# A transformer block, forward and backward: output accumulators without a memset, and a rearranged stage between the forward and the backward attention

## Chip, cores, metric

The kernel runs on one core of one Trainium2 chip. The metric is the time of one execution in device microseconds (us); lower is better. A kernel of 3.0 ms is built from about 72,000 instructions on five engines: TensorE (PE in the profile; its weight loads are PEld), VectorE (DVE), ScalarE (ACT), GpSimd (POOL) and SyncE (SP, which issues transfers).

## The reference

One block of a transformer with adaptive layer norm, for 2048 positions, width 512, 32 heads of 16 and a hidden width of 1792, in bf16. The kernel computes the output and the gradients of nine inputs.

```python
def _A_ref(x, wqkv, wo):                       # attention
    q, k, v = ...                              # (x @ wqkv), 32 heads of 16
    p = _softmax(jnp.einsum('bhqd,bhkd->bhqk', q, k) * 16 ** -0.5)
    return merge_heads(jnp.einsum('bhqk,bhkd->bhqd', p, v)) @ wo

def _B_ref(x, w1, b1, w2, b2):                 # MLP with a squared relu
    r = jnp.maximum(x @ w1 + b1, 0)
    return (r * r) @ w2 + b2

sa, ca, ga, sb, cb, gb = split(_silu(c) @ w_mod, 6)
h = _layernorm(x) * (1 + ca) + sa
x = x + ga * _A_ref(h, A_wqkv, A_wo)
h = _layernorm(x) * (1 + cb) + sb
x = x + gb * _B_ref(h, B_w1, B_b1, B_w2, B_b2)
# returned: x, and the vjp of all this with grad_out
```

The gradients that the change touches are those of w1 and w2 (dW1 and dW2), of b1 (db1: 1792 numbers) and of the modulation vectors sb and cb, which are sums over dW1's blocks.

## The kernel before

It works in three parts. A forward attention, with the MLP of earlier chunks of 512 positions worked in between its units; a middle, in which the last chunk's MLP is done forward and backward and then dW1 and dW2 are formed; and the backward of the attention.

In the forward, a unit is 16 blocks of keys for 512 queries and two heads. Its products are summed in PSUM, the memory that TensorE's matmuls write, in one of two accumulators, which take turns. Both are halves of one tile, `accbank`.

```python
        accbank = accp.tile([P, 2, 2, 4, DH + 1], F32, name="accbank")
        # ...
        def pv(u):
            (qc, g, jp, kb, acc, pu) = u          # acc = accbank[:, n % 2]
            if kb == 0:
                nc.vector.memset(acc, 0.0)                                            # L324
            for a in range(2):
                h = 4 * g + 2 * jp + a
                for sub in range(4):
                    nc.tensor.matmul(acc[:, a, sub, :], lhsT=pu[:, a, sub * P:(sub + 1) * P],
                                     rhs=Vaug[:, kb, h, :], start=False, stop=False,
                                     skip_group_check=True)                           # L328
            if kb < ST - 1:
                return
            for a in range(2):                    # evacuation, after the last block of keys
                nc.vector.reciprocal(self.rl[...], acc[:, a, :, DH])                  # L335
                nc.vector.tensor_tensor(O32[...], acc[:, a, :, 0:DH], ..., ALU.mult)  # L336
```

In the middle, four slices of 128 positions go through `dx` (the gradient in front of the MLP), `fc2` (the MLP's output) and `do` (the gradient in front of the attention's last product). `do` loads a slice of the attention's output, `o32`, through GpSimd's queue and multiplies with it on VectorE.

```python
        def dx(k):
            # ... 14 matmuls
            dx1 = mk.tile([P, D], F32, name="dx1")              # one buffer
            self.ln_bwd_tile(mk, pt[:], xh[:, k, :], gt4[:, k, :], rstd[:, k:k + 1], dx1[:])
            nc.sync.dma_start(tm_v(self.dx1_d)[:, k, :], dx1[:])
            # ... a bf16 copy dxb, stored too; turn_dx(k) transposes it on TensorE
        for k in range(4):
            dx(k)
            if k: turn_dx(k - 1)
            if k > 1: turn_do(k - 2)
            fc2(k)
            if k: do(k - 1)
        # ... dW1 (14 blocks) and dW2 (14 blocks) are worked in between and drained
        self.open_bwd()                     # memsets of 8 masked tiles, first loads of the backward
        fill.drain()
        db1_b = w1p.tile([P, FT], BF16, name="db1_b", bufs=1)
        nc.vector.tensor_copy(db1_b[:], self.db1[:])
        with nc.allow_non_contiguous_dma(reason="column-layout store"):
            nc.gpsimd.dma_start(io["out_5"].rearrange("(t p) -> p t", p=P), db1_b[:])
```

The last line is the store of db1. Its tile has position p on partition p and 14 numbers in a row, and in memory neighbours of such a row are 128 numbers apart: every piece of the transfer is a single number of 2 bytes. It stands at the end of the program text, but it needs only `db1`, and it is issued early, at 1220.7 us (dW2 starts at 1338.0).

A block of dW1, with the sums for the modulation vectors:

```python
            # 64 matmuls into g4 (128 x 512), then the column sums csb of du (one more matmul)
            nc.scalar.copy(csb, csb_ps[:, :P])
            nc.gpsimd.tensor_tensor(t1[:], csb.unsqueeze(1).to_broadcast([P, DT, P]), sbT_b, ALU.mult)
            nc.vector.tensor_tensor(t2[:], g4[:], opcb_b, ALU.mult)
            nc.vector.tensor_tensor(t3[:], g4[:], w1_blk[:], ALU.mult)
            nc.vector.tensor_tensor(dw1[:], t2[:], t1[:], ALU.add)
            nc.gpsimd.dma_start(dw1_v[:, :, ft * P:(ft + 1) * P], dw1[:])
            nc.gpsimd.tensor_tensor(acc_cb[:], acc_cb[:], t3[:], ALU.add)
        # after the 14 blocks: w1 is loaded once more (w1k) for 16 products with csb
```

The softmax here doesn't subtract the row's maximum and nothing guards it: scores larger than these inputs give would overflow.

## Time and profile before

| | us |
|---|---|
| time, median of the runs beside the changed kernel | 3084.86 |
| span of the profiled execution | 3069.6 |
| last exponential of the forward starts | 1148.6 |
| dx stage starts (end of the last product before it) | 1195.0 |
| dW2 starts | 1338.0 |
| backward's first VectorE product starts | 1401.4 |

The last four rows are places in the timeline. Two lines of the page's part on the costliest groups carry the forward. Columns: line, engine, operation, out and in, shapes and count; then busy us and ns of one; then the idle time in front of it and what ended most of that.

```profile
L361 ACT ACTIVATE pu<-st 128x1024 bf16<-128x1024 f32 x1024 | 956.8, 1047 | 84.4 <-PE st L358 80.4
...
L328 PE MATMUL accbank<-Vaug,pu 128*128 128x17 bf16 x8192 | 359.3, 171 | 70.0 <-DVE accbank L324 64.1
```

ScalarE, which sets the pace (between 450 and 750 us it works 285 of 300 us, TensorE 275), stands idle 84.4 us in front of its exponentials, nearly all of it for scores from TensorE. TensorE waits 70.0 us in front of the products into the accumulator, 64.1 of them for the memset.

In the middle, the transfers of the dx stage (view of the transfers, 1195 to 1260 us; columns: what, queue, count, size of one, median us from issue to landing):

```profile
dx_d<-dx SPq DMA_DIRECT2D x4, 256.0 KB, 2.5
...
o<-O_d POOLq DMA_DIRECT2D x3, 256.0 KB, 4.9
...
out_dram<-db_b POOLq DMA_DIRECT2D x1, 3.5 KB, 20.7
```

### The profile page before, as it was taken

What the parts mean: (1) busy time and instruction counts of PE and PEld (TensorE: products, weight loads), DVE (VectorE), ACT (ScalarE), POOL (GpSimd) and SP (SyncE); (2) the same over time, 40 slices, a digit from 0 to 9 for tenths busy, and PEclk for the clock granted to TensorE, in tenths of its full rate; (3) what the DMA queues carried; (4) which work ended last, traced back from release to release, by engine and by line L of the source; (5) the groups of instructions that cost most, each with busy time, mean ns of one, the idle gap of its engine ahead of it and who ended that gap; (6) DMA issues with size and microseconds to landing.
All of it is one profiled execution on the core that took longest, in us unless ns stands there. A gap on an engine that the chain in (4) does not pass through costs nothing. (4 is left out here: it accounts for less than half of the span.)

```text
span 3069.6 us, 72394 instructions
## 1 busy us (share of the span) xinstructions
PE 2731.8 (89%) x29893; PEld 1417.4 (46%) x30394; DVE 1822.7 (59%) x2661; ACT 2240.1 (73%) x3322; POOL 396.6 (13%) x646
## 2 busy tenths in 40 slices
PE   3689889989998988589999999999999999999796
PEld 1345445544444543454444444444444444444343
DVE  5322123322322334367888888888888888888575
ACT  3489999999999984106777777777777777777443
POOL 2343111320221122571000000000000000000000
PEclk7899999999999999799999999999999999999898
DMA  3974230531351136888999999999999999999942
GB/s 128 212 166 121 65 88 25 141 80 37 93 114 48 54 99 183 177 195 164 188 205 200 188 204 189 201 194 192 205 191 206 195 194 206 188 188 180 235 128 72
DMA packets 1306719, 471.12 MB, mean 153 GB/s; under 512 B 1237074, under 2 KB 1269844, under 8 KB 1306388
## 3 DMA queue, kind: packets, MB, share of 16 engines
q1 hardware_dynamic: 1277476, 378.87, 65.7%
q0 software_dynamic: 28384, 86.01, 9.1%
q8 instruction: 238, 3.90, 0.5%
q10 hardware_dynamic: 528, 1.57, 0.1%
q14 instruction: 93, 0.76, 0.1%
HBM read 88.87 MB, written 67.64 MB: 51 GB/s over the span
## 5 line engine op out<-in xcount | busy, mean ns | idle before, releaser
L1185 ACT ACTIVATE pu<-st 128x512 bf16<-128x512 f32 x2048 | 1132.7, 597 | 361.0 <-PE st L1183 297.4
L1190 DVE TENSOR_TENSOR ds<-dp,pu 128x1024 bf16<-128x1024 f32 x1024 | 1208.1, 1219 | 232.9 <-ACT pu L1185 225.0
L361 ACT ACTIVATE pu<-st 128x1024 bf16<-128x1024 f32 x1024 | 956.8, 1047 | 84.4 <-PE st L358 80.4
L1183 PE MATMUL st<-KTm,QTq 128*128 128x512 bf16 x2048 | 778.3, 380 | 13.3 <-ACT pu L1185 11.5
L1133 PEld LDWEIGHTS <-dsT 128*128 128x128 bf16 x8192 | 486.7, 96 | 489.6 <-DMA dsT<-ds 20.2
L1186 PE MATMUL dp<-VTm,dOTq 128*128 128x512 bf16 x1779 | 672.6, 378 | 7.4 <-DVE ds L1190 6.0
L358 PE MATMUL st<-QTm,KTq 128*128 128x512 bf16 x1937 | 596.0, 384 | 57.9 <-issue 17.4
L1133 PE MATMUL accq<-Kg,dsT 128*128 128x16 bf16 x8192 | 493.2, 170 | 27.8 <-DMA dsT<-ds 13.5
L328 PEld LDWEIGHTS <-pu 128*128 128x128 bf16 x8192 | 355.7, 96 | 326.1 <-issue 95.9
L328 PE MATMUL accbank<-Vaug,pu 128*128 128x17 bf16 x8192 | 359.3, 171 | 70.0 <-DVE accbank L324 64.1
L1113 PE MATMUL acckv<-ds,Qg 128*16 128x512 bf16 x2048 | 308.3, 381 | 0.9 <-DVE ds L1190 0.7
L1113 PE MATMUL acckv<-pu,dOg 128*16 128x512 bf16 x2048 | 308.3, 381 | 0.0
L1183 PEld LDWEIGHTS <-QTq 128*128 128x128 bf16 x2048 | 195.9, 96 | 220.8 <-issue 215.8
L358 PEld LDWEIGHTS <-KTq 128*128 128x128 bf16 x2048 | 194.7, 97 | 214.7 <-issue 165.4
L1186 PEld LDWEIGHTS <-dOTq 128*128 128x128 bf16 x2048 | 197.3, 96 | 38.0 <-DVE ds L1190 16.2
L1044 POOL DMA_DIRECT2D wqkv<-in_A_wqkv_dram x1 | 0.8, 788 | 1493.1 <-DMA dsT<-ds 1493.1
L464 DVE TENSOR_SCALAR ev_fm<-pps,bcol 128x512 bf16<-128x512 f32 x60 | 45.0, 750 | 156.7 <-PE pps L456 88.7
L335 DVE RECIPROCAL rl<-accbank 128x4 f32<-128x4 f32 x128 | 23.0, 179 | 175.3 <-PE accbank L328 175.3
L309 POOL DMA_DIRECT2D QTm<-QTq_d x128 | 64.9, 510 | 450.0 <-PE st L358 406.4
L914 DVE TENSOR_SCALAR rT<-pps,bias 128x512 bf16<-128x512 f32 x42 | 31.5, 750 | 116.9 <-PE pps L911 116.7
L922 DVE SCALAR_TENSOR_TENSOR auT<-pps,rT 128x512 bf16<-128x512 f32 x42 | 29.0, 691 | 86.1 <-PE pps L920 71.0
L456 PE MATMUL pps<-xhat1T,wpad 128*128 128x512 bf16 x223 | 78.8, 393 | 0.3 <-issue 0.2
(313 smaller groups left out, 2125.1 us busy)
## 6 DMA issues: line engine op xcount, KB each, us to landing
KTq<-KTq_d POOLq DMA_DIRECT2D x32, 512.0 KB, 3.6
duT_d<-auT POOLq DMA_DIRECT2D x4, 1792.0 KB, 8.2
aT_d<-rT POOLq DMA_DIRECT2D x4, 1792.0 KB, 12.7
QTq_d<-ev_fm SPq DMA_DIRECT2D x32, 128.0 KB, 2.1
QTm<-QTq_d POOLq DMA_DIRECT2D x128, 32.0 KB, 2.0
KTq_d<-ev_fm SPq DMA_DIRECT2D x32, 128.0 KB, 2.0
VTq_d<-vT POOLq DMA_DIRECT2D x4, 1024.0 KB, 6.3
O_d<-O POOLq DMA_DIRECT2D x4, 1024.0 KB, 7.1
```

What stands on the lines that cost most here:

```text
L309: nc.gpsimd.dma_start(QTm[j][32 * j:32 * j + 32, :], self.QTq_d[g, 32 * j:32 * j + 32, 512 * qc:512 * (qc + 1)])
L328: nc.tensor.matmul(acc[:, a, sub, :], lhsT=pu[:, a, sub * P:(sub + 1) * P], rhs=Vaug[:, kb, h, :], start=False, stop=False, skip_group_che ...
L358: nc.tensor.matmul(stt[:, a, :], lhsT=KT[:, kb * P:(kb + 1) * P], rhs=QTm[2 * jp + a][:], start=True, stop=True)
L361: nc.scalar.activation(pu[:], stt[:], ACT.Exp, scale=self.scale)
L456: nc.tensor.matmul(pt[:], lhsT=self.wpads[t][:, kt, g, :], rhs=self.xhat1T[:, kt, s0:s0 + 512], start=(kt == 0), stop=(kt == DT - 1))
L464: nc.vector.tensor_scalar(ev[:], pt[:], bc, None, ALU.add)
L1113: nc.tensor.matmul(acckv[r:r + DH, :], lhsT=T[n][:, ib, col:col + DH], rhs=src[:, a, :], start=(ib == 0), stop=(ib == ST - 1))
L1133: nc.tensor.matmul(accq[:, ib, a, :], lhsT=dsT[:, (i * 2 + a) * 4 + sub, :], rhs=T["K"][:, 4 * c + sub, col:col + DH], start=(c == 0 and i ...
L1183: nc.tensor.matmul(stt[:], lhsT=T["QT"][:, q], rhs=masked["KT"][2 * jp + a][:, c0:c0 + 512], start=True, stop=True)
L1185: nc.scalar.activation(pu[:, a, :], stt[:], ACT.Exp, scale=self.scale)
L1186: nc.tensor.matmul(dp[:, a, :], lhsT=T["dOT"][:, q], rhs=masked["VT"][2 * jp + a][:, c0:c0 + 512], start=True, stop=True)
L1190: nc.vector.tensor_tensor(dsg[:, i], dp[:], pu[:], ALU.mult)
```

## The change

Its intent: take the memset out of the way of the forward's products; keep the operands of dW1 and dW2 resident from the last chunk's MLP on, instead of loading them again; give the dx stage four slices of dx1 and a looser order; do the dW1 epilogue (the work on a block after its matmuls) with per-partition scalars on VectorE and ScalarE, without GpSimd and without the second load of w1; load dW1's blocks three ahead instead of two; and issue the backward's first loads later. The stores of dx1 also move from SyncE's queue to GpSimd's.

```diff
-            if kb == 0:
-                nc.vector.memset(acc, 0.0)
...
-                                     start=False, stop=False, skip_group_check=True)
+                                     start=(kb == 0 and a == 0 and sub == 0), stop=False, skip_group_check=True)
... (loads: resident g_tm and xh2 for dW2 and dW1)
+        nc.sync.dma_start(xh2[:, :st0, :], self.xhat2_d.rearrange("(st p) d -> p st d", p=P)[:, :st0, :])
+        nc.sync.dma_start(g_tm[:, :st0, :], io["grad_out"][0].rearrange("(st p) d -> p st d", p=P)[:, :st0, :])
... (dx stage)
-            dx1 = mk.tile([P, D], F32, name="dx1")
-            self.ln_bwd_tile(mk, pt[:], xh[:, k, :], gt4[:, k, :], rstd[:, k:k + 1], dx1[:])
-            nc.sync.dma_start(tm_v(self.dx1_d)[:, k, :], dx1[:])
+            dx1 = dx1s[:, k, :]
+            self.ln_bwd_tile(mk, pt[:], xh[:, k, :], gt4[:, k, :], rstd[:, k:k + 1], dx1)
+            nc.gpsimd.dma_start(tm_v(self.dx1_d)[:, k, :], dx1)
... (order: dx0 dx1 fc2_0 turn dx2 do0 fc2_1 turn dx3 turn do1 fc2_2 ... in place of the loop; then)
         self.open_bwd()
+        while fill.mark != "half":     # half of dW2
+            fill.next()
+        self.load_bwd()                # the backward's first loads
         fill.drain()
... (dW1: three blocks loaded ahead instead of two; epilogue)
-            nc.gpsimd.tensor_tensor(t1[:], csb.unsqueeze(1).to_broadcast([P, DT, P]), sbT_b, ALU.mult)
-            nc.vector.tensor_tensor(t2[:], g4[:], opcb_b, ALU.mult)
-            nc.vector.tensor_tensor(t3[:], g4[:], w1_blk[:], ALU.mult)
-            nc.vector.tensor_tensor(dw1[:], t2[:], t1[:], ALU.add)
+            for kt in range(DT):
+                nc.scalar.activation(t1[:, kt, :], csb[:], ACT.Copy, scale=self.mod_col(3)[:, kt:kt + 1])
+                nc.vector.scalar_tensor_tensor(dw1[:, kt, :], g4[:, kt, :], self.opcbT[:, kt:kt + 1], t1[:, kt, :], ALU.mult, ALU.add)
+                nc.vector.scalar_tensor_tensor(junk[:], g4[:, kt, :], 1.0, w1_blk[:, kt, :], ALU.mult, ALU.mult,
+                                               accum_out=dcb_part[:, kt, ft:ft + 1])
+                nc.vector.scalar_tensor_tensor(junk2[:], csb[:], 1.0, w1_blk[:, kt, :], ALU.mult, ALU.mult,
+                                               accum_out=dsb_part[:, kt, ft:ft + 1])
... (the w1k loads with their 16 products are gone; in dW2)
-            tmp = sb.tile([P, D], F32, name="g2w2", bufs=1)
+            tmp = sb.tile([P, D], F32, name="g2w2")          # two buffers
```

More of the change, by code (lines that the diff above doesn't have):

```diff
@@ L582, in last_chunk @@
             x0s.append(t)
-        gt4 = e0.tile([P, 4, D], BF16, name="gt4")
-        nc.sync.dma_start(gt4[:], tm_v(io["grad_out"][0]))
         x1 = e0.tile([P, 4, D], F32, name="x1_l")
+        g_tm = e0.tile([P, ST, D], BF16, name="g_tm")
+        xh2 = e0.tile([P, ST, D], BF16, name="xh2")
+        gt4, xh = g_tm[:, st0:, :], xh2[:, st0:, :]
         OT = mk.tile([P, 4, DT, P], BF16, name="fT", bufs=2)
@@ L588, in last_chunk @@
         nc.sync.dma_start_transpose(gT[:], io["grad_out"][0, s0:s0 + 512, :])
+        nc.sync.dma_start(gt4, tm_v(io["grad_out"][0]))
+        nc.sync.dma_start(xh2[:, :st0, :], self.xhat2_d.rearrange("(st p) d -> p st d", p=P)[:, :st0, :])
+        nc.sync.dma_start(g_tm[:, :st0, :], io["grad_out"][0].rearrange("(st p) d -> p st d", p=P)[:, :st0, :])
         bg.take(15)
@@ L597, in last_chunk @@
         nmr = mk.tile([P, 4], F32, name="nmr")
-        xh = mk.tile([P, 4, D], BF16, name="xh2")
         for k in range(4):
@@ L611, in last_chunk @@
         bg.drain()
-        nc.gpsimd.dma_start(tm_v(self.xhat2_d), xh[:])
         xhT = mk.tile([P, 4, DT, P], BF16, name="fT", bufs=2)
@@ L636, in last_chunk @@
         w1p = self.open_pool("dw1", bufs=2)
-        xh2 = w1p.tile([P, ST, D], BF16, name="xh2", bufs=1)
-        nc.sync.dma_start(xh2[:], self.xhat2_d.rearrange("(st p) d -> p st d", p=P))
         fill = Background()
@@ L641, in last_chunk @@
         dxTs, dOpads = {}, {}
+        dx1s = mk.tile([P, 4, D], F32, name="x1")
         def dx(k):
@@ L647, in dx @@
                                  start=(ft == 0), stop=(ft == FT - 1))
-            dx1 = mk.tile([P, D], F32, name="dx1")
-            self.ln_bwd_tile(mk, pt[:], xh[:, k, :], gt4[:, k, :], rstd[:, k:k + 1], dx1[:])
-            nc.sync.dma_start(tm_v(self.dx1_d)[:, k, :], dx1[:])
+            dx1 = dx1s[:, k, :]
+            self.ln_bwd_tile(mk, pt[:], xh[:, k, :], gt4[:, k, :], rstd[:, k:k + 1], dx1)
+            nc.gpsimd.dma_start(tm_v(self.dx1_d)[:, k, :], dx1)
             dxb = mk.tile([P, D], BF16, name="dxb", bufs=2)
-            nc.scalar.copy(dxb[:], dx1[:])
+            nc.scalar.copy(dxb[:], dx1)
             nc.gpsimd.dma_start(tm_v(self.dx1b_d)[:, k, :], dxb[:])
@@ L681, in fc2 @@
             nc.gpsimd.dma_start(tm_v(io["out_0"][0])[:, k, :], o[:])
-        for k in range(4):
-            dx(k)
-            if k:
-                turn_dx(k - 1)
-            if k > 1:
-                turn_do(k - 2)
-            fc2(k)
-            if k:
-                do(k - 1)
+        dx(0)
+        dx(1)
+        fc2(0)
+        turn_dx(0)
+        dx(2)
+        do(0)
+        fc2(1)
+        turn_dx(1)
+        dx(3)
+        turn_do(0)
+        do(1)
+        fc2(2)
+        turn_dx(2)
+        turn_do(1)
+        fc2(3)
+        do(2)
         self.close_pool("mlp_f")
-        g_tm = self.open_pool("dw2", bufs=2)
-        fill.add(self.gen_dw2(g_tm))
-        fill.take(16)
+        w2p = self.open_pool("dw2", bufs=2)
+        fill.add(self.gen_dw2(w2p, g_tm))
+        fill.take(4)
         turn_dx(3)
+        fill.take(4)
         turn_do(2)
-        fill.take(4)
         do(3)
-        fill.take(24)
+        fill.take(32)
         turn_do(3)
@@ L718, in gen_dw1 @@
         dw1_v = io["out_4"].rearrange("(kt p) f -> p kt f", p=P)
-        db1_bc = sb.tile([P, F], F32, name="db1_bc", bufs=1)
-        acc_cb = sb.tile([P, DT, P], F32, name="acc_cb", bufs=1)
-        nc.gpsimd.memset(acc_cb[:], 0.0)
-        opcb_b = self.opcbT[:].unsqueeze(2).to_broadcast([P, DT, P])
-        sbT_b = self.mod_col(3).unsqueeze(2).to_broadcast([P, DT, P])
+        dcb_part = sb.tile([P, DT, FT], F32, name="dcb_part", bufs=1)
+        dsb_part = sb.tile([P, DT, FT], F32, name="dsb_part", bufs=1)
+        nc.vector.memset(dcb_part[:], 0.0)
+        nc.vector.memset(dsb_part[:], 0.0)
         blks = []
         def load(ft):
-            r = sb.tile([P, ST, P], BF16, name="du_blk", bufs=3)
-            nc.sync.dma_start_transpose(r[:], self.duT_d[ft])
-            w = sb.tile([P, DT, P], BF16, name="w1_blk", bufs=3)
+            r = sb.tile([P, ST, P], BF16, name="du_blk", bufs=4)
+            cuts = (0, ST - 4, ST) if ft < 3 else (0, ST)
+            for (a, b) in zip(cuts, cuts[1:]):
+                nc.sync.dma_start_transpose(r[:, a:b, :], self.duT_d[ft, :, a * P:b * P])
+            w = sb.tile([P, DT, P], BF16, name="w1_blk", bufs=4)
             with nc.allow_non_contiguous_dma(reason="256B runs"):
                 nc.gpsimd.dma_start(w[:], w1_v[:, :, ft * P:(ft + 1) * P])
-            diag = sb.tile([P, P], F32, name="diag", bufs=3)
+            diag = sb.tile([P, P], F32, name="diag", bufs=4)
             nc.gpsimd.tensor_scalar(diag[:], self.ident_f[:], db1[:, ft:ft + 1], 1.0, ALU.mult, ALU.mult)
             blks.append((r, w, diag))
-        load(0)
-        load(1)
+        for ft in range(3):
+            load(ft)
         for ft in range(FT):
-            if ft + 2 < FT:
-                load(ft + 2)
+            if ft + 3 < FT:
+                load(ft + 3)
             du, w1_blk, diag = blks[ft]
@@ L750, in gen_dw1 @@
             nc.tensor.matmul(csb_ps[:, :P], lhsT=self.ones_f[:], rhs=diag[:], start=True, stop=True)
-            csb = db1_bc[:, ft * P:(ft + 1) * P]
-            nc.scalar.copy(csb, csb_ps[:, :P])
-            t1 = sb.tile([P, DT, P], F32, name="t1", bufs=1)
-            nc.gpsimd.tensor_tensor(t1[:], csb.unsqueeze(1).to_broadcast([P, DT, P]), sbT_b, ALU.mult)
-            t2 = sb.tile([P, DT, P], F32, name="t2", bufs=1)
-            nc.vector.tensor_tensor(t2[:], g4[:], opcb_b, ALU.mult)
-            t3 = sb.tile([P, DT, P], F32, name="t3", bufs=1)
@@ L758, in gen_dw1 @@
-            nc.vector.tensor_tensor(t3[:], g4[:], w1_blk[:], ALU.mult)
-            dw1 = sb.tile([P, DT, P], BF16, name="dw1")
-            nc.vector.tensor_tensor(dw1[:], t2[:], t1[:], ALU.add)
+            csb = sb.tile([P, P], F32, name="csb")
+            nc.scalar.copy(csb[:], csb_ps[:, :P])
+            t1 = sb.tile([P, DT, P], F32, name="t1")
+            dw1 = sb.tile([P, DT, P], BF16, name="dw1")
+            for kt in range(DT):
+                nc.scalar.activation(t1[:, kt, :], csb[:], ACT.Copy, scale=self.mod_col(3)[:, kt:kt + 1])
+                nc.vector.scalar_tensor_tensor(dw1[:, kt, :], g4[:, kt, :], self.opcbT[:, kt:kt + 1], t1[:, kt, :], ALU.mult, ALU.add)
+                junk = sb.tile([P, P], F32, name="junk")
+                nc.vector.scalar_tensor_tensor(junk[:], g4[:, kt, :], 1.0, w1_blk[:, kt, :], ALU.mult, ALU.mult,
+                                               accum_out=dcb_part[:, kt, ft:ft + 1])
+                junk2 = sb.tile([P, P], F32, name="junk")
+                nc.vector.scalar_tensor_tensor(junk2[:], csb[:], 1.0, w1_blk[:, kt, :], ALU.mult, ALU.mult,
+                                               accum_out=dsb_part[:, kt, ft:ft + 1])
@@ L761, in gen_dw1 @@
             with nc.allow_non_contiguous_dma(reason="256B runs"):
                 nc.gpsimd.dma_start(dw1_v[:, :, ft * P:(ft + 1) * P], dw1[:])
-            nc.gpsimd.tensor_tensor(acc_cb[:], acc_cb[:], t3[:], ALU.add)
-        nc.vector.tensor_reduce(self.dcb_col[:], acc_cb[:], axis=AX.X, op=ALU.add)
-        dsb_part = sb.tile([P, DT, len(chunks(F, 512))], F32, name="dsb_part", bufs=1)
-        nc.vector.memset(dsb_part[:], 0.0)
-        for kt in range(DT):
-            w1k = sb.tile([P, F], BF16, name="w1k", bufs=1)
-            nc.gpsimd.dma_start(w1k[:], w1_v[:, kt, :])
-            for ci, (f0, fw) in enumerate(chunks(F, 512)):
-                junk = sb.tile([P, 512], F32, name="t2", bufs=1)
-                nc.vector.scalar_tensor_tensor(junk[:, :fw], db1_bc[:, f0:f0 + fw], 1.0, w1k[:, f0:f0 + fw], ALU.mult, ALU.mult,
-                                               accum_out=dsb_part[:, kt, ci:ci + 1])
+        nc.vector.tensor_reduce(self.dcb_col[:], dcb_part[:], axis=AX.X, op=ALU.add)
@@ L774, in gen_dw1, with gen_dw2 @@
         nc.vector.tensor_reduce(self.dsb_col[:], dsb_part[:], axis=AX.X, op=ALU.add)
-    def gen_dw2(self, sb):
+    def gen_dw2(self, sb, g_tm):
         nc, io = self.nc, self.io
@@ L780, in gen_dw2 @@
         nc.gpsimd.memset(dgb[:], 0.0)
-        g_tm = sb.tile([P, ST, D], BF16, name="g_tm", bufs=1)
-        nc.sync.dma_start(g_tm[:], io["grad_out"][0].rearrange("(st p) d -> p st d", p=P))
         b2_b = sb.tile([1, D], BF16, name="b2_b", bufs=1)
@@ L806, in gen_dw2 @@
             nc.gpsimd.dma_start(io["out_6"][ft * P:(ft + 1) * P, :], dw2[:])
-            tmp = sb.tile([P, D], F32, name="g2w2", bufs=1)
+            tmp = sb.tile([P, D], F32, name="g2w2")
             nc.vector.tensor_tensor(tmp[:], pt[:], w2_blk[:], ALU.mult)
             nc.gpsimd.tensor_tensor(dgb[:], dgb[:], tmp[:], ALU.add)
-            if ft == 0:
+            if ft == FT // 2:
+                yield ("half", 0)
                 pt = self.dps.tile([P, 512], F32, name="dps")
@@ L1055, in open_bwd, with load_bwd @@
         self.qp = self.open_pool("p5q", bufs=2, side="right")
+    def load_bwd(self):
+        nc = self.nc
         self.T0, pieces = self.load_group(0)
```

## The prediction

> **What bounds the kernel now.** I read the page's slices first. The span of 3069.6 us has three parts: a forward attention up to about 1150 us, a middle of about 250 us (the last chunk's MLP, then dW1 and dW2), and an attention backward from 1398 us on. The change touches nothing after 1398 us except the way that part is entered, so 1670 us of the span should stay. Then I cut the middle with the view of windows (stretch, its length, then each engine's busy us and instructions, granted TensorE clock, DMA share):
>
> ```profile
> 1150.00:1195.00 45.00, 42.43 (x212) 19.35 (x215) 22.33 (x65) 22.66 (x34) 8.25 (x13) 1.00 0.33 101
> 1195.00:1254.00 59.00, 34.01 (x153) 14.95 (x155) 18.83 (x55) 13.84 (x27) 15.02 (x23) 0.80 0.77 195
> 1254.00:1338.00 84.00, 64.14 (x952) 60.95 (x951) 41.86 (x61) 7.30 (x20) 67.70 (x74) 0.90 0.97 223
> 1338.00:1398.00 60.00, 53.55 (x236) 23.65 (x240) 34.76 (x68) 0.27 (x1) 39.04 (x49) 0.97 0.75 179
> ```
>
> From 1195 us the first engine, TensorE, works 34 of 59 us and 64 of 84 us, and the clock falls to 0.80 and 0.90: this is where time lies open. Next the waits of TensorE and ScalarE, first inside the forward, then between 1195 and 1398 us:
>
> ```profile
> PE accbank L328 <- DVE accbank L324: 64.1, 63, 6.0
> ACT pu L361 <- PE st L358: 80.4, 77, 7.0
> ...
> PE tp L576 <- ACT dxb L652: 19.4, 2, 17.3
> PE dps L745 <- DMA du_blk<-duT_d: 13.0, 4, 6.8
> PE tp L576 <- DVE dOpad L1017: 6.4, 3, 2.7
> PE dps L802 <- DVE g2w L808: 4.8, 3, 2.6
> PE dps L745 <- DVE t L758: 4.6, 7, 3.0
> ```
>
> The first line is what the memset seems to cost: 63 waits, 64.1 us. The forward is paced by ScalarE's exponentials (285 of 300 us busy between 450 and 750 us), with TensorE close behind at 275, so only what ScalarE loses counts. The timeline around one change of accumulator shows what the wait is made of:
>
> ```profile
> 494.70 0.22 DVE L336 TENSOR_TENSOR O<-accbank,rl 128x64 f32<-128x64 f32 x1
> 494.83 0.18 DVE L335 RECIPROCAL rl<-accbank 128x4 f32<-128x4 f32 x1
> 495.04 0.22 DVE L336 TENSOR_TENSOR O<-accbank,rl 128x64 f32<-128x64 f32 x1
> 495.37 0.17 DVE L324 MEMSET accbank<- 128x136 f32 x1
> 495.60 0.35 PE L328 MATMUL accbank<-Vaug,pu 128*128 128x17 bf16 x8 [0.73 <-DVE accbank L324]
> ...
> 496.70 13.93 ACT L361 ACTIVATE pu<-st 128x1024 bf16<-128x1024 f32 x15 [0.65 <-PE st L358]
> ```
>
> The memset is only the end of a queue on VectorE: it stands behind the evacuation of the other accumulator. Evacuation ends at 495.26, memset at 495.54, matmul at 495.60.
>
> [...] So the start matmul must still wait for the evacuation of the *other* half. The trace agrees: none of the 8192 accumulator matmuls overlaps in time any of the 256 evacuation instructions. [...] The trace fits: the db1 store, 3.5 KB in 2-byte pieces, was issued at 1220.74 and landed after 20.75 us, and the du_blk transpose beside it (issued 1219.16) took 22.5 us where the median is 6.5. [...] The trace: 289 ns at 128 columns, 690 at 512, thus about 155 ns fixed.
>
> **The change part by part.**
> *Memset.* I took, for each of the 63 later memsets, the end of the last evacuation and the end of the memset. In 54 the difference is 0.28 us; in the rest 0.38 to 1.85 us, where another Vector instruction slipped between. ScalarE's idle stretch just after is between nothing and 7 us. The smallest of the difference, TensorE's wait and ScalarE's idle, summed, is 24 us. The evacuation itself (two reciprocals and two multiplies, about 1 us) stays in front of the matmul. Expected: 22 us, not 64.
> *dx stage (1195 us on).* Today the 17.3 us and 2.1 us waits come from dx1 having a single buffer: VectorE may not write the next dx1 until the store of the last has landed:
>
> ```profile
> 1223.80 3.19 PE L646 MATMUL pps<-W1mT,auT 128*128 128x512 bf16 x14
> 1244.32 0.61 PE L576 MATMUL tp<-ident,dxb 128*128 128x128 bf16 x4 [17.33 <-ACT dxb L652]
> 1242.86 0.75 DVE L531 SCALAR_TENSOR_TENSOR dx<-lnb_t,rstd,lnb_gp 128x512 f32<-128x512 f32 x1 [24.08 <-DMA dx_d<-dx]
> ```
>
> Four slices of dx1 take that wait away, and the new order puts 3 to 8 us of matmuls between a Vector chain and its consumer. TensorE's own work is four times dx 3.0, fc2 3.2, do 0.9, the two transposes 1.4: 34 us. But the db1 store remains, and the o32 loads, one buffer, stand on the same queue: if one is issued behind it, VectorE stops in order at the product with o32. I allow 7 us for that.
> *dW1.* TensorE: 64 matmuls take 3.59 us, the column-sum matmul 0.28, so 3.87 a block, 54 us for 14. Today a steady block takes 4.24 us, since VectorE waits for the GpSimd product and its next instruction runs 1.74 us instead of 0.69 beside GpSimd:
>
> ```profile
> 1308.20 3.75 PE L745 MATMUL dps<-du_blk,xh 128*128 128x128 bf16 x64 [2.97 <-DVE t L758]
> 1312.44 3.75 PE L745 MATMUL dps<-du_blk,xh 128*128 128x128 bf16 x64 [0.22 <-DVE t L758]
> 1309.25 1.74 DVE L760 TENSOR_TENSOR dw<-t,t 128x512 bf16<-128x512 f32 x1 [1.10 <-POOL t L754]
> ```
>
> The new epilogue is 12 Vector instructions of 128 columns. Back to back they start about 0.21 us apart (0.29 less the overlap of 0.08): 2.6 us a block, plus about 0.9 for column sum, copy and first scale on ScalarE; that is 3.5 to 3.7 us against TensorE's 3.87, just under. If each waits another 0.1 us it is 3.8 + 0.9 = 4.7 and VectorE sets the pace. Loads of du_blk come earlier (three blocks, old columns first; xhat2 and grad already resident, so 4 MB no longer stand in front). What stays: GpSimd's eight memsets of the backward's masked tiles, 14.1 us in one piece from 1285.7 to 1299.7, behind the landing of dOTq. They no longer stop a GpSimd product, but they hold the dW1 stores (two buffers) and the w1 loads. I allow 9 us of TensorE wait, 2 more for a slow clock after it.
> *dW2.* 240 matmuls of 0.213 us are 51 us; today 60. The w1k loads and their 16 Vector instructions (idle 4.6, 2.1 and 3.1 us on VectorE) go away, and g2w gets a second buffer. Against that the backward's first loads, about 2.3 MB, now fall in its second half, beside DMA at 0.75: I allow 4 us.
> *Sum of the middle.* 34 + 54 + 51 = 139.5 us of TensorE, plus 7 + 1.5 (clock) + 11 + 4 + 3 (rest) = 166 us, against 1398 − 1195 = 203 us: 37 to 40 us gained. With the forward's 22 us: about 61 us, 2.0%, on 3085: 3023.
>
> **The rivals.** *A: no wait at all is left at the accumulator.* [...] ScalarE's whole idle after the changes, 56 us, can go, and the time is about 2990. [...] *B: one outage replaces another.* The db1 store or the masked memsets stop TensorE as long as the dx1 store did; then the middle gains only 20 us and the time is 3043. For it: both are still there[...]. *C: VectorE becomes the bound of dW1*, 4.5 us or more a block instead of 4.24: 14 times 0.4 to 0.7 lost against my 3.87, about 6 to 10 us: 3031. For it: four times as many instructions. *D: everything in the middle flows*, 150 us: 3008. *E: the later backward loads make the backward start late*, up to 10 us: 3033.
>
> **Range and chances.** The parts spread by about 6 us in the forward and 14 in the middle; A, at one in seven, stretches it downwards, B and C upwards. The range is 2992 to 3054. The 2% line is at 3023, on my estimate, so faster and same are even; slower needs a loss that no view shows.
>
> **What would show each step.** Right: accumulator waits of TensorE stay, now on the evacuation at L336, at about 40 us; no wait on the dx1 store; no GpSimd product in dW1, blocks about 3.9 us apart; dW2 near 52 us; the backward begins near 1338 us and lasts as long as before. Wrong: accumulator waits near zero (A); a single wait of over 10 us in dx or dW1 behind a load of o32, a dW1 store or the memsets (B); dW1 blocks of 4.4 us with VectorE busy throughout (C); a gap in front of the backward's first matmul (E).

That the start flag can stand in for the memset was argued; what shows it is that the kernels with the flag give right results (e1_memset_off_only and c_after_again below). That the matmul would still wait for the other half rests on the absence of overlaps in the trace alone. The slow clock that is allowed for after a wait can be read in the kernel before: after the wait of 17.3 us the granted clock was 0.50 from 1242 to 1250 us, 0.79 to 1254 and 1.00 to 1262. For the stop of VectorE at the product with o32, the trace after has 14.94 us.

## The result

| | before | after |
|---|---|---|
| median of 4 runs, us | 3084.86 | 3040.24 |
| lowest to highest, us | 3082.49 to 3086.32 | 3028.17 to 3041.62 |
| last exponential of the forward starts | 1148.6 | 1115.8 |
| dx stage starts | 1195.0 | 1162.5 |
| dW2 starts | 1338.0 | 1292.2 |
| backward's first VectorE product starts | 1401.4 | 1349.4 |
| end of the profiled execution | 3069.6 | 3026.2 |

The ratio is 0.9847, 95% interval 0.9822 to 0.9873: 1.5% faster, within 2%. A ratio here is the mean time of one kernel's runs over that of the other's in the same rounds, so it is not quite the ratio of the medians. The profiled execution is the fastest of its kernel in both cases, some 13 us under the median; differences of places are therefore taken between profiled executions.

From these places: the forward gave 32.8 us. From there to the backward's first product another 19.2 us were gained (52.0 less 32.8). Then 8.6 us were lost up to the end (52.0 less 43.4). That last number isn't a property of the change: from the first product to the end the fourteen profiled executions, whose kernels share this code, took between 1668.2 us (the kernel before) and 1678.1 us, in no order that follows their edits.

**The forward after.** The groups that answer to those shown of before:

```profile
L359 ACT ACTIVATE pu<-st 128x1024 bf16<-128x1024 f32 x1024 | 955.2, 1050 | 51.1 <-PE st L356 46.3
...
L326 PE MATMUL accbank<-Vaug,pu 128*128 128x17 bf16 x8192 | 358.5, 171 | 43.2 <-DVE O L334 35.0
```

ScalarE's idle time falls by 33.3 us, which is the forward's gain. TensorE still waits 43.2 us, and what ends 35.0 of them is now L334, the evacuation. The timeline around one change of accumulator (start us, length, then the instruction; in brackets the idle time in front and what ended it):

```profile
481.67 0.18 DVE L333 RECIPROCAL rl<-accbank 128x4 f32<-128x4 f32 x1
...
482.13 0.22 DVE L334 TENSOR_TENSOR O<-accbank,rl 128x64 f32<-128x64 f32 x1
482.26 0.17 DVE L333 RECIPROCAL rl<-accbank 128x4 f32<-128x4 f32 x1
482.47 0.23 DVE L334 TENSOR_TENSOR O<-accbank,rl 128x64 f32<-128x64 f32 x1
482.75 0.35 PE L326 MATMUL accbank<-Vaug,pu 128*128 128x17 bf16 x8 [0.46 <-DVE O L334]
```

The matmul into the one half starts 0.05 us after the evacuation of the other half has ended (482.47 + 0.23 = 482.70). Over all 63 changes, the first matmul came 1.16 us after the previous accumulator's last one before the change and 0.89 us after it (medians).

**The middle after**, cut at the same places (view of windows; columns: stretch, length, then busy us and instructions of TensorE, its weight loads, VectorE, ScalarE, GpSimd; TensorE's granted clock as a share of full speed, mean busy share of the DMA engines, GB/s):

```profile
1117.00:1162.50 45.50, 42.74 (x219) 19.52 (x220) 22.53 (x67) 22.70 (x34) 7.52 (x12) 1.00 0.51 158
1162.50:1219.00 56.50, 36.64 (x206) 18.10 (x207) 21.44 (x66) 15.97 (x31) 21.01 (x32) 0.85 1.05 188
1219.00:1292.00 73.00, 58.09 (x900) 56.57 (x899) 39.30 (x271) 21.87 (x68) 35.64 (x42) 0.91 0.94 207
1292.00:1346.00 54.00, 52.06 (x239) 23.52 (x242) 22.40 (x54) 1.55 (x5) 32.78 (x42) 1.00 0.76 171
```

dx and dW1 together take 129.5 us, before 143; dW2 takes 54, before 60, and is now full. In dx and dW1 TensorE still stands still for about 35 us. Three lines of its waits name nearly all of that (in all, times, longest):

```profile
PE tp L574 <- DVE dOpad L1019: 19.1, 2, 16.2
PE dps L760 <- DVE junk L769: 7.5, 1, 7.5
PE dps L755 <- DVE junk L769: 6.9, 4, 2.5
```

The wait on dx1 is gone, and a new one of 16.2 us stands in its place. The timeline shows where the two longest come from:

```profile
1188.19 1.16 POOL L718 DMA_DIRECT2D out_dram<-db_b  x1
...
1190.24 0.57 POOL L990 DMA_DIRECT2D o<-O_d  x1
...
1213.70 0.69 DVE L1002 TENSOR_TENSOR lnb_junk<-dOp_t,o 128x512 f32<-128x512 bf16 x1 [14.94 <-DMA o<-O_d]
...
1216.26 1.01 PE L574 MATMUL tp<-ident,dOpad 128*128 128x128 bf16 x8 [16.21 <-DVE dOpad L1019]
...
1238.27 7.04 POOL L499 MEMSET KTm<- 128x2048 bf16 x4 [3.47 <-DMA dOTq_d<-dOTq]
1245.25 7.05 POOL L499 MEMSET VTm<- 128x2048 bf16 x4
...
1256.81 0.35 DVE L767 SCALAR_TENSOR_TENSOR dw<-dps,opcbT,t 128x128 bf16<-128x128 f32 x1 [13.94 <-DMA out_dram<-dw]
...
1259.48 0.80 PE L760 MATMUL dps<-diag,ones_f 128*128 128x128 f32 x2 [7.54 <-DVE junk L769]
```

The first story: the db1 store is issued at 1188.19 and lands 24.5 us later, at 1212.7. The load of o32, issued 2 us after it, lands at 1213.6, after 23.4 us (median of these loads in the kernel before: 3.9); all seven transfers that GpSimd issued between 1189.3 and 1197.9 landed between 1213.4 and 1216.3, in the order of their issue. VectorE stops for 14.94 us in front of the product that needs it, and TensorE for 16.21 us in front of the transpose that needs VectorE. The second: while GpSimd clears the eight masked tiles from 1238.3 to 1252.3 it issues no dW1 store (the next one comes at 1252.25); VectorE waits 13.94 us for such a store before it writes the next dw; and TensorE's next product into dps waits 7.54 us for VectorE's L769, which reads dps. The view of transfers, from 1162 to 1262 us, has the first story in numbers:

```profile
o<-O_d POOLq DMA_DIRECT2D x3, 256.0 KB, 8.0
...
out_dram<-db_b POOLq DMA_DIRECT2D x1, 3.5 KB, 24.5
```

Undisturbed blocks of dW1 follow each other in 3.85 us, where they took 4.24 before:

```profile
1280.64 3.74 PE L755 MATMUL dps<-du_blk,xh 128*128 128x128 bf16 x64
...
1281.57 0.35 DVE L767 SCALAR_TENSOR_TENSOR dw<-dps,opcbT,t 128x128 bf16<-128x128 f32 x1 [1.87 <-ACT t L766]
1281.84 0.28 DVE L769 SCALAR_TENSOR_TENSOR junk<-dps,w_blk 128x128 f32<-128x128 f32 x1
...
1282.05 0.29 DVE L772 SCALAR_TENSOR_TENSOR junk<-csb,w_blk 128x128 f32<-128x128 f32 x1
...
1282.26 0.35 DVE L767 SCALAR_TENSOR_TENSOR dw<-dps,opcbT,t 128x128 bf16<-128x128 f32 x1
...
1284.49 3.74 PE L755 MATMUL dps<-du_blk,xh 128*128 128x128 bf16 x64
```

Three VectorE instructions take about 0.69 us by their starts (1281.57 to 1282.26), so 2.7 us a block, and VectorE waits for ScalarE at the start of the block: it is no bound here.

The later backward loads are one thing that didn't take place. The text places them after half of dW2, but in the trace they are issued between 1238 and 1257 us, within dW1. So they did not crowd dW2's second half, and no gap opened in front of the backward.

### The profile page after: what moved, and what is told of

It reads as the page before. It is cut to its first block, busy times and chain, and to the rows that moved or that the text cites. A ratio compares the mean times of both kernels' runs of the same rounds, so it can differ in the third digit from the quotient of the medians. Undisturbed runs are those within 1.5% of the kernel's fastest.

```text
span 3026.2 us, 72535 instructions
## 1 busy us (share of the span) xinstructions
PE 2726.1 (90%) x29894; PEld 1416.7 (47%) x30394; DVE 1797.7 (59%) x2804; ACT 2257.3 (75%) x3378; POOL 364.2 (12%) x616
## 5 line engine op out<-in xcount | busy, mean ns | idle before, releaser
L1138 PEld LDWEIGHTS <-dsT 128*128 128x128 bf16 x8192 | 487.6, 96 | 493.9 <-DMA dsT<-ds 21.5
L326 PE MATMUL accbank<-Vaug,pu 128*128 128x17 bf16 x8192 | 358.5, 171 | 43.2 <-DVE O L334 35.0
L1191 PEld LDWEIGHTS <-dOTq 128*128 128x128 bf16 x2048 | 197.4, 96 | 37.9 <-DVE ds L1195 16.2
## 6 DMA issues: line engine op xcount, KB each, us to landing
aT_d<-rT POOLq DMA_DIRECT2D x4, 1792.0 KB, 12.8
```

The lines of the kernel that those rows point to most:

```text
L1138: nc.tensor.matmul(accq[:, ib, a, :], lhsT=dsT[:, (i * 2 + a) * 4 + sub, :], rhs=T["K"][:, 4 * c + sub, col:col + DH], start=(c == 0 and i ...
L1191: nc.tensor.matmul(dp[:, a, :], lhsT=T["dOT"][:, q], rhs=masked["VT"][2 * jp + a][:, c0:c0 + 512], start=True, stop=True)
```

## The experiments

Twelve runs in three calls; each call on one chip, with seven runs of the kernel before beside them (median 3076.18, 3081.47 and 3085.52 us). Ratios are against those. A ratio has an interval of about 0.0025 to each side, some 8 us, so two ratios are told apart only from a difference of about 0.0035 (11 us) on. The texts and the labels say bank for the place of a tile in PSUM; no trace shows banks.

### 1. The memset alone, and everything but the memset

```diff
# e1_memset_off_only: the kernel before, with the first hunk of the change alone
-            if kb == 0:
-                nc.vector.memset(acc, 0.0)
-                                     start=False, ...
+                                     start=(kb == 0 and a == 0 and sub == 0), ...
# e2_memset_back: the changed kernel with that hunk undone
```

> The kernel before with the start flag in place of the memset and nothing else. Theory: the matmul still waits for the evacuation of the other half of its bank, so only the memset and what stood between goes. In the traces of before and after ScalarE's idle time at the 63 changes of accumulator fell by 27.5 us and the forward by 32.8; alone it should give 24 to 33 us (3052 to 3061), waits of TensorE on the evacuation of about 37 us, and a middle unchanged within 3 us. Rival A (no wait left): 56 us or more, no such waits. Rival that the gain came from other parts of the change: under 15 us.

> The changed kernel with the memset put back and nothing else. If the parts add up, it loses the 24 to 33 us that the memset alone costs, and lands at 3064 to 3073; against the kernel before that leaves 12 to 20 us, which is what the middle of the change is worth. If the parts hide one another, it loses under 15 us.

| run | median us | ratio | interval | last forward exponential, against before | from there to the backward, us |
|---|---|---|---|---|---|
| e1_memset_off_only | 3050.77 | 0.9915 | 0.989 to 0.9939 | -31.8 | 254.9 |
| e2_memset_back | 3058.82 | 0.9945 | 0.9922 to 0.9968 | +1.3 | 232.6 |
| (before) | 3076.18 | | | 0 | 252.8 |
| (after, its own rounds) | 3040.24 | 0.9847 | 0.9822 to 0.9873 | -32.8 | 233.6 |

Both kernels give right results. The two parts add up within the noise: the memset alone is worth 26 us (0.0085 of 3076), everything else 17 us (0.0055 of 3076), and the sum, 43 us, lies between the 47 and 42 us (0.0153 and 0.0137) that the whole change gave in its two measurements. So the forward gave a little more than the prediction's 22 us, and the middle less than half of its 37 to 40.

### 2. Is the wait that remains at the accumulator due to the shared tile?

The tile is split in two, one for each accumulator. The second tile is paid for with one of the three buffers of the MLP's matmul outputs; the control makes that payment alone. The changed kernel ran once more beside them.

```diff
# e3c_mps2: the control
-        self.mps = self.open_pool("mps", bufs=3, space=PSUM)
+        self.mps = self.open_pool("mps", bufs=2, space=PSUM)
# e3_two_banks: that, and
-        accbank = accp.tile([P, 2, 2, 4, DH + 1], F32, name="accbank")
+        accbank = [accp.tile([P, 2, 4, DH + 1], F32, name=f"accbank{i}") for i in range(2)]
-                acc = accbank[:, n % 2]
+                acc = accbank[n % 2]
```

> The changed kernel as it is, on the chip of this call, as the control for the next runs: ratio to the kernel before 0.982 to 0.987. In the profiled run so far the backward was 5.6 us longer than in the kernel before; if that is scatter, it will be otherwise here (other profiled runs: between 0 and 9 us longer).

> Control for the next run: the changed kernel with two instead of three rotating banks for the background's matmuls, which frees one bank that is left empty. Loses 0 to 15 us, in the forward and in the dx stage, since a matmul there may have to wait for the evacuation of the one before last.

> As the control with two rotating banks, and the two accumulators each in a bank of its own. Theory: what is left of the waits at the accumulator (37 us of TensorE, 34 of ScalarE's idle) is the evacuation of the other half of the same bank. In two banks it goes: waits under 6 us, the forward 20 to 30 us shorter than in the control. Rival: the matmul waits for VectorE because it must (its own accumulator, two units back, is evacuated late); then the waits stay over 20 us.

| run | median us | ratio | interval | last forward exponential, against before |
|---|---|---|---|---|
| c_after_again | 3039.99 | 0.9863 | 0.9827 to 0.99 | -28.3 |
| e3c_mps2 | 3039.73 | 0.985 | 0.9823 to 0.9877 | -30.0 |
| e3_two_banks | 3014.87 | 0.9779 | 0.9754 to 0.9805 | -60.4 |

The same two groups of the page, of e3_two_banks:

```profile
L359 ACT ACTIVATE pu<-st 128x1024 bf16<-128x1024 f32 x1024 | 949.8, 1057 | 30.9 <-PE st L356 28.4
...
L326 PE MATMUL accbank<-Vaug,pu 128*128 128x17 bf16 x8192 | 358.2, 171 | 0.0
```

TensorE's wait in front of the accumulator is zero, ScalarE's idle time falls by another 20 us, and the time by 22 to 26 us (0.0071 to 0.0084). The median time between the accumulators falls from 0.89 to 0.57 us. By the times of the profile, 464 of the 8192 accumulator matmuls now overlap an evacuation; before the change, after it and in the control none does. The buffer given up costs nothing that the runs show, and the repeat of the changed kernel agrees with the first measurement. So the wait that the change left was that of one half for the evacuation of the other half. Why one tile keeps the wait is not shown: the runs compare one tile with two.

### 3. The db1 store and the masked memsets, in the changed kernel

```diff
# e4_db1_rows: the changed kernel; db1 is turned on TensorE and stored as 14 rows of 256 bytes
+        db_ps = self.dps.tile([P, 512], F32, name="dps")
+        nc.tensor.matmul(db_ps[0:FT, 0:P], lhsT=self.db1[:], rhs=self.ident_f[:], start=True, stop=True)
+        db1_b = w1p.tile([FT, P], BF16, name="db1_b", bufs=1)
+        nc.scalar.copy(db1_b[:], db_ps[0:FT, 0:P])
+        nc.gpsimd.dma_start(io["out_5"].rearrange("(t p) -> t p", p=P), db1_b[:])
         fill.take(32)
...     (the store in single numbers at the end is gone)
# e5_spread: the changed kernel; the eight memsets come one at a time between pieces of dW1 and dW2
-                nc.gpsimd.memset(t[:], 0.0)          # in make_masked
+        for n in ("KT", "VT"):                       # after open_bwd
+            for j in range(4):
+                nc.gpsimd.memset(self.masked[n][j][:], 0.0)
+                fill.take(16)
# e6_rows_spread: both
```

> The changed kernel, but db1 is turned by TensorE and stored as 14 rows of 256 bytes instead of 1792 pieces of 2 bytes. Theory: that store (24.5 us to landing) delays the landing of everything issued behind it, among it the third o32 load (23.4 us), for which VectorE waits 14.9 us and TensorE 16.2 us. Without it: o32 lands in 5 to 8 us, the 16 us wait shrinks to under 4, time down by 11 to 16 us (about 3026). Rival: the DMA queues are simply full there (3 MB of du_blk, aT and duT in flight); then o32 still takes over 15 us and the time falls by under 4 us. Second rival: the time won is given back at the masked memsets, which then hold the dW1 stores longer: 4 to 8 us remain.

> The changed kernel with GpSimd's eight masked memsets put one to a dW1 block instead of all eight together. Theory: the 14.1 us that they take in one piece hold the dW1 stores, VectorE waits 13.9 us for a free dw1 tile, TensorE 7.5 us at once and some 4 after; spread, these waits fall under 3 us in all and the time by 7 to 11 us (3029 to 3033). Rival: spread memsets slow VectorE in every block[...] (1.74 us beside GpSimd instead of 0.69 in the kernel before), and the blocks grow from 3.9 to over 4.3 us: nothing gained.

> The changed kernel with both repairs of the middle, the db1 store in rows and the masked memsets spread over the dW1 blocks. If the two waits are independent their gains add: 10.8 us (rows) and 5.8 us (spread) as measured one by one, 14 to 19 us below the changed kernel, about 3015 where before is 3076. If one hides the other, under 12 us.

| run | median us | ratio | interval | last forward exponential to the backward, us |
|---|---|---|---|---|
| e4_db1_rows | 3019.0 | 0.9812 | 0.9792 to 0.9832 | 216.9 |
| e5_spread | 3023.61 | 0.9828 | 0.981 to 0.9847 | 231.3 |
| e6_rows_spread | 3020.08 | 0.979 | 0.9766 to 0.9815 | 223.9 |

In e4 the store lands in 4.7 us instead of 24.5, and the load of o32 in 6.3 (view of transfers, 1190 to 1260 us):

```profile
o<-O_d POOLq DMA_DIRECT2D x2, 256.0 KB, 6.3
...
out_dram<-db_b POOLq DMA_DIRECT2D x1, 3.5 KB, 4.7
```

and its waits of TensorE in the middle read

```profile
PE dps L756 <- DVE junk L770: 7.1, 3, 3.6
PE dps L761 <- DVE junk L770: 7.0, 1, 7.0
PE tp L574 <- DVE dOpad L1020: 4.9, 2, 3.6
```

The wait on dOpad falls from 19.1 to 4.9 us, the one behind the memsets stays at 7.0, and the time is 11 to 16 us lower than the changed kernel's (0.9812 against 0.9847 and 0.9863), by itself just clear of the noise. The long wait of the dx stage was the db1 store's. One thing to note for this and every other run with the rows: the edit changes two things at once, the pieces of the store and its place. In e4 it is issued at 1209.8 us, after the last load of o32 at 1206.5, where in the changed kernel it came at 1188.2, ahead of two of them. So the runs show what it is worth not to have that store in that place; they do not show that rows in the old place would do as well. For that speaks the store's own duration, which was between 19.0 and 29.0 us in single numbers wherever the trace has it, and between 4.7 and 8.1 us in rows.

In e5 the single wait of 7.5 us behind the memsets is gone and the 16.9 us wait on dOpad stays, as it should. But other waits of dW1 grow to 9.7 us, and the time falls by only 6 to 11 us, inside what two measurements can differ by. In e6 both long waits are gone, and smaller ones take their place: 12.5 us on VectorE in dW1 in six pieces, 5.3 us for a ScalarE copy, 3.0 us for du_blk. Its time is 18 to 22 us below the changed kernel's (14 to 19 were expected if the gains add), but its interval overlaps e4's. So it is not shown that the memsets cost time; e5's interval leaves room for some 16 us, and what they cost beside the rows stays open.

### 4. Was it the single buffer of dx1, in the kernel before?

The prediction put the 17.3 us wait of the kernel before down to dx1's single buffer. The same rows store, in the kernel before, tests that: the single buffer stays.

```diff
# e7_before_rows: the kernel before; the edit of e4_db1_rows and no other
```

> The kernel before, with only the db1 store written as 14 rows of 256 bytes. Question: how much of the kernel before's 17.3 us and 2.1 us waits in the dx stage was already this store, and not the single dx1 buffer. Theory (the store holds back whatever lands behind it, and the single buffer only let it reach the chain): the dx1 store stands behind the db1 store in landing, so the 24 us wait of VectorE falls to under 10, and the time falls by 10 to 18 us. Rival (the single buffer itself is the cause): the wait on the dx1 store stays over 15 us and the time moves by under 4 us.

Measured: 3067.54 us, ratio 0.9951, interval 0.9929 to 0.9973, so 15 us faster than the kernel before. The wait on the dx1 store and what followed from it:

```profile
1229.61 0.75 DVE L531 SCALAR_TENSOR_TENSOR dx<-lnb_t,rstd,lnb_gp 128x512 f32<-128x512 f32 x1 [9.22 <-DMA dx_d<-dx]
...
1231.07 0.40 PE L576 MATMUL tp<-ident,dxb 128*128 128x128 bf16 x4 [2.46 <-ACT dxb L652]
```

VectorE's wait fell from 24.08 to 9.22 us and TensorE's from 17.33 to 2.46, with the single buffer in place. In the kernel before, the dx1 store in question was issued at 1223.2 us, 2.5 us after the db1 store; that one landed at 1241.5, and VectorE went on at 1242.9. In e7 the db1 store comes at 1249.9, after the stores of dx1 that were waited for. Nor were the transfers late because there was too much to move. In the kernel before, while that wait lasted (view of windows, columns as above):

```profile
1231.00:1242.00 11.00, 0.00 (x0) 0.00 (x0) 0.00 (x0) 0.00 (x0) 0.00 (x0) 0.51 0.08 0
```

For 11 us no engine works, the DMA engines are busy for 0.08 of the time, and next to no bytes move. So the db1 store, issued 2.5 us ahead of it, had made the dx1 store late (24.08 us of waiting, against 9.22 in e7), and the single buffer passed this on to TensorE (17.33 us, against 2.46). Of the 9.22 us that stay with the buffer in e7, 3.6 pass before the store is even issued, at 1223.97: in SyncE's queue it stands behind three transposed loads of du_blk, which took 12.5 us to issue. The theory put on record holds for these stores and for the o32 load, and this is the study's main reading: getting that store out of the way saves 15 us in the kernel before and 11 to 16 in the changed one. The four slices of dx1 took the late store off the path, but not what made it late, and the o32 load, which has one buffer, was late in its place.

### 5. Two parts of the change undone, one at a time

```diff
# e9_old_core: the changed kernel with the old core of the dW1 epilogue
+            nc.gpsimd.tensor_tensor(t1[:], csb[:].unsqueeze(1).to_broadcast([P, DT, P]), sbT_b, ALU.mult)
+            nc.vector.tensor_tensor(t2[:], g4[:], opcb_b, ALU.mult)
+            nc.vector.tensor_tensor(t3[:], g4[:], w1_blk[:], ALU.mult)
+            nc.vector.tensor_tensor(dw1[:], t2[:], t1[:], ALU.add)
+            nc.gpsimd.tensor_tensor(acc_cb[:], acc_cb[:], t3[:], ALU.add)
...     (in place of the scale on ScalarE and two of the three products; the one into dsb_part stays)
# e8_loads_late: the changed kernel; two loads back at their old places
-        nc.sync.dma_start(xh2[:, :st0, :], ...)      # beside the last chunk's first loads
-        nc.sync.dma_start(g_tm[:, :st0, :], ...)
+        nc.sync.dma_start(xh2[:, :st0, :], ...)      # at the opening of dW1's pool
+        nc.sync.dma_start(g_tm[:, :st0, :], ...)     # at the opening of dW2's pool
```

> The changed kernel with the core of the old dW1 epilogue put back: one GpSimd product and 512-wide Vector instructions in each block in place of the per-partition scalars. Theory (GpSimd's product makes VectorE wait and slows it, and stands behind the masked memsets in GpSimd's queue): blocks 4.2 us apart instead of 3.85, and the product of one or two blocks waits for the 14 us of memsets, so +5 to +20 us against the changed kernel. Rival (the epilogue is not the bound, TensorE and the DMA waits are): within 4 us.

> The changed kernel with the loads of the old chunks' xhat2 and grad_out (2 MB) back at their old places at the start of dW1 and dW2. Theory (early residence takes them out of the way of the du_blk and weight loads): new waits on DMA in dW1 or dW2, +3 to +12 us. Rival (DMA has room there, residence is worth nothing by itself): within 3 us.

Measured: e9_old_core 3039.29 us, ratio 0.9862 (0.9836 to 0.9888); e8_loads_late 3036.53 us, ratio 0.9849 (0.9826 to 0.9872). Neither differs from the changed kernel's 0.9847 and 0.9863.

For e8 nothing speaks against the rival: no new wait of TensorE on these loads appears, and the early loads are worth nothing that shows, though the clock would not show a few us. For e9 the trace shows the mechanism that the theory named (waits of VectorE, 1205 to 1312 us):

```profile
DVE dw L772 <- POOL t L766: 21.5, 8, 12.5
```

VectorE waits 21.5 us for GpSimd's product, 12.5 of them in one piece behind the masked memsets, and the last five steps from block to block of dW1 take 26.9 us together, where four profiled executions with the changed kernel's own dW1 (after, c_after_again, e3c_mps2 and e3_two_banks) take 20.0 to 22.1. But dW1 as a whole, from its first matmul to its last, took 101.8 us, and in those four it took 94.0, 93.1, 98.6 and 101.6. So 5 to 7 us are there in the trace and the clock doesn't confirm them: the theory's 5 to 20 us is not shown, and only a gain of more than some 13 us from the part undone is excluded.

### 6. Both losses out

```diff
# e11_banks_rows: the changed kernel with the edits of e3_two_banks and of e4_db1_rows
```

> The changed kernel with the two remaining losses taken out together: each accumulator half in its own bank (with a single-buffered matmul output in the MLP to pay for the bank), and the db1 store as rows. If the two are independent, as forward and middle are: 23 us and 14 us off the changed kernel, ratio to the kernel before about 0.974, near 3003 us. If the gain of the rows comes only by chance of order, about 3015, as with the two banks alone.

Measured: 2998.85 us (2994.85 to 3006.77), ratio 0.9727, interval 0.9703 to 0.9751; the result is correct. That is 2.7% under the kernel before, 84 us, and the best kernel. The db1 edit gives 16 us on top of the two tiles (0.9779 less 0.9727), with intervals that don't overlap: the third measurement of the store, and it agrees with the other two. In the profile the accumulator's products wait 0.0 us again:

```profile
L359 ACT ACTIVATE pu<-st 128x1024 bf16<-128x1024 f32 x1024 | 950.5, 1057 | 34.4 <-PE st L356 32.1
...
L326 PE MATMUL accbank<-Vaug,pu 128*128 128x17 bf16 x8192 | 358.5, 171 | 0.0
```

## Why the prediction was right or wrong

The time was right: 3023 was predicted, with 2992 to 3054 as its range, and 3040.24 came. It was right with two errors that partly cancel (the forward gave more than was said, the middle less than half), so that the time came inside the range is in part luck. The result lies where the prediction's own rival B had put it: "the middle gains only 20 us and the time is 3043". B's sign came too: a single wait of 16.2 us behind a load of o32 in place of the 17.3 us behind the dx1 store.

**The memset: right, and slightly too small.** The prediction said 22 us and not 64. The memset alone is worth 26 us in the timed runs; ScalarE's idle time fell by 33.3 us in the profiled one. The mechanism is as it was put: the evacuation stays in front of the matmul, 0.27 us less lies between the accumulators (1.16 less 0.89), and the wait is now on the evacuation, 35.0 us where about 40 was expected. The term was mis-sized for a visible reason: it took the smallest of three quantities at each change, summed 24, and rounded down. The time between the accumulators, summed over the 63 changes, falls by 26.6 us (109.4 to 82.8), and the last exponential comes 24 to 33 us earlier in the profiled executions of the changed kernel and of those that differ from it only in the middle.

**Rival A: excluded for this kernel; its prize was there to be had.** With both halves in one tile TensorE still waited 43.2 us in front of these products, 35.0 of them for the evacuation. Two tiles brought that to 0.0 and gave 22 to 26 us more. The prediction had put A's gain 34 us above its own forward term (56 against 22).

**The dx stage: the step that failed.** "Today the 17.3 us and 2.1 us waits come from dx1 having a single buffer." Experiment 4 shows that the buffer alone does not make them: with that buffer kept and the db1 store out of the way the wait is 2.46 us. It took a late store as well, so four slices of dx1 ended the wait on dx1 and left the cause, which stopped the o32 load instead. The prediction had seen that store and its 20.75 us, and had even named the o32 load as the place where it could show again, but it allowed 7 us there; 19.1 came. Its own reading of the trace, that a transfer beside the store took 22.5 us where the median is 6.5, should have been applied to the dx1 store as well: that store has a median of 2.5 us in this stage, it was issued 2.5 us after db1's, and VectorE's wait for it was 24.08.

**dW1: the pace right, the outages too small.** 3.87 us a block was predicted, 3.85 came, with 2.7 us of VectorE against a predicted 2.6; rival C is excluded. The masked memsets stayed, as foreseen: 7.5 us of waiting behind them in one piece, and 6.9 us in four shorter waits on VectorE, against 9 in all. In experiment 3 the long one is gone and the shorter ones have grown to 9.7 us.

**dW2: right.** Some 52 us was predicted for its work, 54 came for the window, of which 52.06 busy. The 4 us allowed for the crowding of loads did not come, since the loads were not in fact later; for the same reason rival E could not arise. The reason of the prediction fell there, and its number stood.

**The sum of the middle.** Predicted for dx and dW1: 34 + 54 + 7 + 1.5 + 11 = 107.5 us; measured 129.7 (1162.5 to 1292.2). The 22 us between them: 12.8 are the dOpad wait and a small one beside it (19.1 + 0.7, against 7); 5.8 the waits in dW1 (7.5 + 6.9 + 0.4, against 9); 3.4 TensorE's busy time (94.9 at a granted clock of 0.88, against 88 and the 3.5 that were allowed for the clock). dW2 and the rest came out 4 us better (54, against 51 + 4 + 3). That leaves 18 us, which is the difference between the predicted 37 and the measured 19, and it excludes rival D, a middle of 150 us: it took 184.

**What stays open.** The middle's 17 us are not traced to one part of the change. The early loads by themselves give nothing that shows (e8), the new dW1 core at most some 13 us (e9). What was changed in one piece and not tested is the dx stage's order, buffers and store queue, the loading of dW1's blocks three ahead (the first three in two pieces), the second load of w1 with its 16 products, and the second g2w buffer. This new loading may be worth much of the 17 us, which no run tests: TensorE's 13.0 us of waits on du_blk in the kernel before are gone in the changed one, also in e8, where the early loads are undone. The second load of w1 and the g2w buffer are read as dW2's 6 us, because the waits that they ended are gone, but no run separates them. Nor is it settled how much the masked memsets cost once the db1 store is out of the way, nor how much of that store's gain comes from its rows and how much from its later place.

## What to carry to other kernels

A wait names the buffer that is missing, not the event that is late: ask first why the transfer that should free the buffer landed late. Here one store of 3.5 KB held back what was issued behind it, in the kernel before through dx1 (24.08 us of VectorE's waiting) and in the changed one through o32 (14.94 us), and storing it later and in rows gave about 15 us in each of three kernels, where in the changed kernel, which has four buffers of dx1, the wait had only moved. When a wait is made of a queue, as at the accumulator, price only the part that is removed, and then look at whether the rest can be removed at its root: here it was the tile that the two accumulators shared, and splitting it was worth 22 to 26 us, as much as the memset (26 us).
